# One-core attention with soft experts: row sums folded by a turned VectorE reduce and joined by eight narrow products, with all items placed anew

## The chip, the cores and the metric

One core of one Trainium2 chip runs the whole program. The metric is the device time of one execution in microseconds (us); the median of three runs of the kernel before is 463.78 us (462.85 to 466.7).

## The reference

The inputs are q, k, v of 4 batches x 8 heads x 768 positions x 64, a projection to 6 bits, and the weights of a soft mixture of experts.

```python
q_bits = (einsum('bhsd,dk->bhsk', q, proj) > 0); k_bits = ...      # six bits: a bucket number
mask = q_bucket[:, :, :, None] == k_bucket[:, :, None, :]
scores = where(mask, (q @ k.T) / sqrt(D), -1e9)
attn = exp(scores - max(scores, axis=-1)); attn = attn / (sum(attn, axis=-1) + 1e-9)
x = (attn @ v).transpose(0, 2, 1, 3).reshape(B * S, H * D)          # 3072 x 512
logits = x @ phi                                                    # 32 slots
slot_input = softmax(logits, axis=0).T @ x
slot_out[e] = relu(slot_input[e] @ w1[e]) @ w2[e]                   # 8 experts, 4 slots each
out = softmax(logits, axis=1) @ slot_out
```

The change is about one line of it: `sum(attn, axis=-1) + 1e-9`, the row sums of each head, and the division by them.

## The kernel before, in words

Attention works head by head (32 heads), with keys on the partitions and queries along the free axis, so a row sum is a sum over partitions and over the six key tiles. For head `h` and key tile `i`, in this flow:

- `smax` (TensorE, L692) makes a first product of bits for the mask and the row maximum; `most` (VectorE, L701 and L704) reduces it out of PSUM to maxima `mx`. The PSUM pool `p_sm` of `smax` has two tiles, so `smax` can be two tiles ahead of `most` and no more. A `most` takes one such tile: 512 columns, or two times 256.
- `shift` (VectorE, L730 to L733) turns the maxima of a head into 12 columns of the tile `mz_wide`, and `shift_rows` (TensorE transpose, L740) turns that tile so that ScalarE and a DMA can put it into the operands of the scores.
- `scores` (TensorE, L755) and `exps` (ScalarE, L761) make the exponentials `pt`; three tiles of PSUM hold scores.
- `acc` (GpSimd, L769 and L772) adds up the exponentials of the six key tiles to `acc`, 128 x 768 per head: five additions per head. What is left of the row sum is a sum over the 128 partitions.
- `av` (TensorE, L782) multiplies exponentials and values. Its products are 32 wide in the array, four beside each other; one `av(h, i)` is eight instructions, because an f32 product is two passes.

Two heads form a pair. For pair `p` = (h, h+1) with h even, before:

- `pair_sum` (L794): four products of `ones` (128 x 32) with the two `acc` tiles, 384 columns each, eight instructions side by side as in `av`; then ScalarE adds epsilon into the tile `sm` (L797).
- `pair_turn`: VectorE transposes `sm` in 32 x 32 blocks (L801) and takes the reciprocal of 12 columns (L803).
- `pair_rec`: VectorE transposes the reciprocals back over 384 columns (L807), and four small ScalarE copies (L811) lay them out as `r` for the two heads.
- `pair_log` (TensorE, L819) makes the logits of the pair, `pair_add` (VectorE, L830 and L832) multiplies them with the turned-back reciprocals and adds them up; `pair_x` (VectorE, L841 and L842), twice per pair, turns a head's output and scales it by `r`.

`pair_sum`, `bits`, `pair_log`, `shift` and `pair_x` share two PSUM tiles, `p_mi`. The last pair (heads 30 and 31) takes other functions, `one_sum` (L850) to `one_x`, which sum each head by itself.

The order of the work is written out by hand. Each item (one call such as `av(14, 2)`) has a place, a number: a general place per kind in `WHEN`, counted in key tiles from the start of its head (six per head, so 12 per pair), and places of their own for the first heads in `FIRST` and for the last ones in `LAST`. All items are sorted by place and issued in that order; each engine then runs its instructions strictly in the order of issue. A place is no time: it only decides what stands before what on each engine. After the attention come the experts (L1210 to L1289), which have an order of their own that no place touches.

Of the kernel before, what the change touches and what calls it, by code (L numbers as in the profile page):

```python
# [45 lines left out]
WHEN = {'load': -19.3468,  # L46
 'bits': -14.4383,
 'bits_over': -14.2584,
 'split_hi': -10.9429,
 'split_lo': [-7.9471, -10.3929],  # L50
 'spread': [[-8.8667, -8.6015, -5.9161, -4.1148], [-9.3276, -9.194, -9.0297, -9.106]],
 'load_v': [-2.0731, 0.6585],
 'smax': [[-4.9459, -4.5996, -4.5074, -3.5395, -3.8379, -3.601, -3.1412, -4.194, -2.497, -2.6603, -2.5816, -2.8044], [-7.8073, -7.4789, -7.2707, -6.1194, -5.7614, -1.4853, -1.3463, -5.5604, -1.6131, -0.5258, -0.2808, -0.8326]],
 'scores': [[5.3442, 7.1595, 7.6417, 4.7818, 4.7301, 7.7385, 7.8065, 6.1303, 7.7833, 7.8637, 8.1476, 7.0548], [2.9827, 3.0435, 3.3599, 2.8156, 6.1475, 3.339, 3.3842, 3.4177, 4.8664, 6.3101, 6.3175, 5.5112]],
 'shift': [-2.1809, 1.1337],
 'shift_rows': [-2.0508, 1.4963],
 'acc': [[8.2045, 8.8273, 9.2763, 9.7038, 11.6083], [5.3851, 6.3996, 7.6087, 9.3787, 10.196]],
 'av': [[8.1798, 8.2669, 9.6327, 9.6481, 9.703, 9.8775], [7.1277, 7.2791, 9.6226, 9.7634, 9.8792, 10.1433]],
 'pair_sum': 21.5121,
 'pair_turn': 22.2861,  # L60
 'pair_rec': 22.5427,
 'pair_log': 21.6476,
 'pair_x': [25.4827, 31.869],
 'pair_add': 22.6152,
 'batch_both': 23.9517,
 'batch_max': 28.4907,
 'batch_exp': 29.0783,
 'batch_turn': 33.1628,
 'batch_scale': 38.996,
 'batch_slots': 33.3856,  # L70
 'batch_weigh': 33.2973,
 'batch_share': 33.7326,
 'batch_arrange': 33.8276,
 'load_weights': 32.5147,
 'most': [[-4.2417, -4.1358, -3.3957, -3.7458, -3.1116, -3.8628, -2.4263, -2.4256, -2.7421], [-6.3291, -5.9099, -5.7091, -4.4019, -0.3972, -4.3936, -1.1706, 1.0908, -0.2473]],
 'exps': [[6.8148, 8.101, 6.373, 5.0098, 8.3028, 7.1088, 8.7019, 8.5894, 7.3908], [3.1649, 3.733, 2.9391, 6.3842, 3.7337, 3.5784, 5.6014, 6.3847, 6.3149]]}
# [1278 lines left out]
```

## Time and profile before

| | |
|---|---|
| median of three runs | 463.78 us (462.85 to 466.7) |
| span of the profiled execution | 459.7 us |
| busy: PE / PEld / DVE / ACT / POOL | 444.7 / 277.2 / 336.8 / 275.1 / 350.9 us |
| attention, pair after pair | 54.3 to 388.7 us of the span |
| last pair, and the last logits | 388.7 to 409.5 us |
| experts | 409.5 to 459.7 us |

PE is TensorE's products, PEld its weight loads, DVE is VectorE, ACT ScalarE, POOL GpSimd. A row of the profile gives a line of the kernel, the engine, the operation, the tiles out<-in with their shapes and a count. Busy time of PE is that of pipelined products whose ends are modelled: a PE that is always busy is not yet one at its peak. A time in brackets is the idle time of the engine before the instruction, and behind the arrow stands what ended it.

### The profile page before, as it was taken

Reading aid. Unit: us, or ns where it says so; the run is one execution under the profiler, and the core shown is the slowest. Engines: PE = TensorE matmul, PEld = TensorE weight load, DVE = VectorE, ACT = ScalarE, POOL = GpSimd, SP = SyncE. Lnnn points to the kernel's source line nnn. Section 1 sums busy time; section 2 is a strip of 40 time slices with the busy share of each in tenths; the row PEclk is TensorE's granted clock in tenths of the full one; section 3 lists DMA queues with packets and bytes.
Section 4 is the critical chain, followed back from the end, with each engine's and each line's share of the span. In section 5 each row is a group of like instructions: output and inputs, shape, how many; then the busy total and the mean of one; then the engine's idle time right before and its main releaser. Section 6 shows DMA issues by size and latency. Waiting matters only on the chain. (4 is left out here: it accounts for less than half of the span.)

```text
span 459.7 us, 10940 instructions
## 1 busy us (share of the span) xinstructions
PE 444.7 (97%) x4109; PEld 277.2 (60%) x4109; DVE 336.8 (73%) x670; ACT 275.1 (60%) x572; POOL 350.9 (76%) x220
## 2 busy tenths in 40 slices
PE   8999999999999999999999999999999999879993
PEld 6755656575757575656565656565665754343682
DVE  5967787777798978787889878787988780773142
...
GB/s 207 137 151 148 165 134 153 131 197 164 211 159 190 183 163 209 163 202 171 201 167 187 175 187 190 178 202 169 196 177 112 98 227 404 315 336 355 412 310 274
DMA packets 37704, 93.20 MB, mean 203 GB/s; under 512 B 7106, under 2 KB 13380, under 8 KB 37652
## 3 DMA queue, kind: packets, MB, share of 16 engines
...
q14 instruction: 20, 0.16, 0.1%
q0 software_dynamic: 32, 0.07, 0.0%
HBM read 52.76 MB, written 6.29 MB: 128 GB/s over the span
## 5 line engine op out<-in xcount | busy, mean ns | idle before, releaser
L772 POOL TENSOR_TENSOR acc<-acc,pt 128x768 f32<-128x768 f32 x125 | 229.5, 1838 | 17.4 <-ACT pt L761 11.7
L761 ACT ACTIVATE pt<-st 128x512 f32<-128x512 f32 x288 | 158.2, 598 | 57.2 <-PE st L755 52.8
L755 PE MATMUL st<-XY 128*128 128x512 f32 (+1 forms) x768 | 170.9, 342 | 1.1 <-ACT pt L761 1.1
L704 DVE TENSOR_REDUCE mx<-smx 128x1 f32<-128x512 f32 x192 | 129.3, 687 | 53.0 <-PE smx L692 51.0
L782 PE MATMUL av<-pt,v 128*32 128x384 f32 x1536 | 137.6, 489 | 0.0
L755 PEld LDWEIGHTS st<-XY 128*128 128x128 f32 x768 | 122.2, 190 | 20.0 <-ACT pt L761 3.9
L692 PE MATMUL smx<-XY 96*128 96x256 f32 (+1 forms) x384 | 116.6, 356 | 0.8 <-DVE XY L632 0.3
L692 PEld LDWEIGHTS smx<-XY 96*128 96x128 f32 x384 | 67.7, 190 | 34.8 <-DVE mx L704 12.5
L782 PEld LDWEIGHTS av<-pt,v 128*32 128x32 f32 x1536 | 45.8, 109 | 68.6 <-issue 66.5
L769 POOL TENSOR_TENSOR acc<-pt 128x768 f32<-128x768 f32 x32 | 58.7, 1833 | 12.1 <-ACT pt L761 12.1
L701 DVE TENSOR_REDUCE mx<-smx 128x2 f32<-128x512 f32 x96 | 65.5, 683 | 2.7 <-PE smx L692 2.2
L596 POOL TENSOR_TENSOR w<-raw,w 128x768 fp32r<-128x768 f32 x16 | 35.5, 2222 | 3.8 <-ACT w L592 2.2
L786 ACT COPY avs<-av 128x384 f32<-128x384 f32 x32 | 15.3, 479 | 35.0 <-PE av L782 35.0
L797 ACT ACTIVATE sm<-mi,eps 128x384 f32<-128x384 f32 x15 | 8.7, 582 | 32.0 <-PE mi L794 32.0
L592 ACT CAST w<-raw 128x768 fp32r<-128x768 f32 x30 | 23.6, 834 | 2.4 <-DMA XY<-w 2.1
L609 ACT CAST XY<-w 64x768 fp32r<-64x768 f32 x30 | 23.5, 830 | 0.0
L596 DVE TENSOR_TENSOR w<-raw,w 128x768 fp32r<-128x768 f32 x14 | 16.8, 1203 | 2.7 <-ACT w L592 1.6
L842 DVE TENSOR_TENSOR xq<-mi,r 128x384 f32<-128x384 f32 x30 | 16.7, 558 | 2.1
L841 DVE STREAM_TRANSPOSE mi<-avs 128x384 f32<-128x384 f32 x30 | 17.4, 580 | 0.0
L801 DVE STREAM_TRANSPOSE sm<-sm 128x384 f32<-128x384 f32 x15 | 8.6, 572 | 10.9 <-ACT sm L797 10.9
L1263 PE MATMUL qs<-w 128*32 128x128 f32 x464 | 15.4, 274 | 0.8 <-issue 0.8
L1263 PEld LDWEIGHTS qs<-w 128*32 128x32 f32 x464 | 13.9, 110 | 2.5 <-issue 2.4
...
## 6 DMA issues: line engine op xcount, KB each, us to landing
...
```

Source lines behind the costliest of these rows:

```text
L592: nc.scalar.copy(st[h]["w4"][:, 2 * x], st[h]["raw", x])
L596: (nc.vector if h > 2 and x == 0 else nc.gpsimd).tensor_tensor(out=w[:, 2 * x + 1], in0=st[h]["raw", x], in1=w[:, 2 * x], op=ALU.subtract)
L609: nc.scalar.copy(s["Y"][0:64, x], s["w4"][0:64, 2 * x])
L692: nc.tensor.matmul(pt[:, o:o + b - a], s["Y"][0:96, 0, t * P:(t + 1) * P], s["Y"][0:96, 1, a:b], start=True, stop=True)
L701: nc.vector.tensor_reduce(out=mx[:, n - 1:n + 1], in_=s["sm_ps", n - 1].rearrange("p (a x) -> p a x", a=2), axis=AX.X, op=ALU.max)
L704: nc.vector.reduce_max(out=mx[:, n:n + 1], in_=s["sm_ps", n], axis=AX.X)
L755: nc.tensor.matmul(pt[:, o:o + b - a], x[:, 1, i * P:(i + 1) * P], x[:, 0, a:b], start=first, stop=not first)
L761: nc.scalar.activation(s["P", n // 4][:, 512 * u:512 * u + 512], s["st_ps", n - (n % 4 == 2)], AF.Exp, scale=D ** -0.5)
L769: nc.gpsimd.tensor_tensor(out=s["acc"], in0=pr[:, 0:S], in1=pr[:, S:2 * S], op=ALU.add)
L772: eng.tensor_tensor(out=s["acc"], in0=s["acc"], in1=pr[:, a * S:(a + 1) * S], op=ALU.add)
L782: nc.tensor.matmul(s["av"][2 * e + 32 * c:2 * e + 32 * c + 32, 0:HC], s["v"][:, i, e:e + 32], pr[:, o + c * HC:o + (c + 1) * HC], start=(i ...
L1263: nc.tensor.matmul(pos[i][32 * j:32 * j + 32, 0:w], hTs[g][:, f, 32 * j:32 * j + 32], wt[1, x, 2 * g + f // 4, j][:, (f % 4) * HM + o:(f % ...
```

## The change

The row sums of heads 0 to 29 go another way. A new item `part(h)`, once per head, lets VectorE reduce the 128 x 768 tile `acc` with its 32 x 32 blocks turned: each of the four groups of 32 partitions is summed up, and what comes out is 128 x 24. It is written into columns 12 to 59 of `mz_wide`, 24 for the even and 24 for the odd head; `shift_rows` goes on turning all 72 columns of that tile. `pair_sum` then joins the four groups with a matrix `quarter` (128 x 32, four identities on top of each other): four products of 24 columns and four of 12, which stand in three groups of 12 columns in PSUM and need no ScalarE. `pair_turn` adds epsilon out of PSUM and takes the reciprocals of 36 columns at once; `pair_rec` keeps its transpose back, and its four ScalarE copies and the first transpose go. `add_quarter` makes `quarter` once, in three small GpSimd additions. Some small tiles are put together or share a name.

```diff
+    def add_quarter():
+        nc.gpsimd.tensor_tensor(out=quarter, in0=ident[:, 0:32], in1=ident[:, 32:64], op=ALU.add)
+        for n in (64, 96):
+            nc.gpsimd.tensor_tensor(out=quarter, in0=quarter, in1=ident[:, n:n + 32], op=ALU.add)
...
     def shift(h):
         s = st[h]
-        mz = mz_wide
+        mz = mz_wide[:, 0:2 * NT]
...
-        nc.tensor.transpose(pt[0:72, 0:P], s["mz"], ident)
+        nc.tensor.transpose(pt[0:72, 0:P], mz_wide, ident)
...
+    def part(h):
+        q = st[h - h % 2]
+        q["parts"] = mz_wide[:, 2 * NT:10 * NT].rearrange("p (a j) -> p a j", a=2)
+        nc.vector.tensor_reduce(out=q["parts"][:, h % 2], in_=st[h]["acc"].rearrange("p (j x) -> p j x", x=32),
+                                axis=AX.X, op=ALU.add, apply_transpose=True)
+
     def pair_sum(h):
+        n = NT * 2
         pt = p_mi.tile([P, 512], F32, name="mi")
-        for a in range(2):
-            for c in range(2):
-                r = 64 * a + 32 * c
-                nc.tensor.matmul(pt[r:r + 32, 0:HC], ones, st[h + a]["acc"][:, c * HC:(c + 1) * HC],
-                                 start=True, stop=True)
+        for g in range(4):
+            nc.tensor.matmul(pt[32 * g:32 * g + 32, 0:2 * n].rearrange("p (a j) -> p a j", a=2), quarter,
+                             st[h]["parts"][:, :, g % 2 * n:g % 2 * n + n], start=True, stop=True)
+        for g in range(4):
+            nc.tensor.matmul(pt[32 * g:32 * g + 32, 2 * n:3 * n], quarter,
+                             st[h]["parts"][:, g // 2, g % 2 * n:g % 2 * n + n], start=True, stop=True)
+        st[h]["sum"] = pt[:, 0:3 * n]
+
+    def pair_turn(h):
+        n = NT * 2
+        r = dp.tile([P, 3 * n], F32, name="r", bufs=1)
+        nc.vector.tensor_scalar_add(r, st[h]["sum"], EPS)
+        nc.vector.reciprocal(out=r, in_=r)
+        st[h]["r"] = r[:, 0:2 * n].rearrange("p (a j) -> p a j", a=2)
+        st[h]["rt"] = r[:, 2 * n:3 * n]
+
+    def pair_rec(h):
         st[h]["rs"] = dp.tile([P, HC], F32, name="sm", bufs=1)
-        nc.scalar.activation(st[h]["rs"], pt[:, 0:HC], AF.Identity, bias=eps)
-
-    def pair_turn(h):
-        tt = st[h]["rs"]
-        nc.vector.transpose(tt, tt)
-        r = st[h]["rt"] = dp.tile([P, NT * 2], F32, name="rt", bufs=1)
-        nc.vector.reciprocal(out=r, in_=tt.rearrange("p (j x) -> p j x", x=32)[:, :, 0])
-
-    def pair_rec(h):
-        r = st[h]["rt"]
-        nc.vector.transpose(st[h]["rs"], r[:, :, None].broadcast_to([P, NT * 2, 32]))
-        r2 = st[h]["r"] = dp.tile([P, 2, NT * 2], F32, name="r", bufs=1)
-        for a in range(2):
-            for x in range(2):
-                nc.scalar.copy(r2[64 * x:64 * x + 64, a], r[64 * a:64 * a + 64])
+        nc.vector.transpose(st[h]["rs"], st[h]["rt"][:, :, None].broadcast_to([P, NT * 2, 32]))
...
+        if h < BH - 2:
+            at(s0 + WHEN["part"][x], part, h)
```

All places in `WHEN`, `FIRST` and `LAST` are other numbers. Sorted, they give this order around a pair, with pair (12, 13) as the example:

```
before  TensorE: pair_sum(12) bits(18) av(14,2) pair_log(12) av(14,3) av(14,4) av(14,5) shift_rows(16)
        VectorE: most(16,8) most(16,10) bits_over(18) shift(16) pair_turn(12) pair_rec(12) pair_add(12)
after   TensorE: av(14,2) pair_sum(12) av(14,3) bits(18) av(14,4) pair_log(12) av(14,5) smax(17,0,0) shift_rows(16)
        VectorE: part(13) most(16,10) pair_turn(12) pair_rec(12) bits_over(18) most(16,8) shift(16) pair_add(12)
```

The `part` of an even head stands around the six `av` of an odd head that follow one another, or some items behind them; that of an odd head stands at the end of the next long stretch of `smax` and `scores` (8 of the 14 from head 3 on, just ahead of `av(even, 0)`) or a little later, ahead of its `pair_sum`. Over the whole list TensorE changes between full-width and 32-wide products 119 times before and 116 times after.

## Rows read from the trace of the kernel before

**Rows 1.** The page: the span, then busy us, share and instructions per engine.
```profile
span 459.7 us, 10940 instructions
...
PE 444.7 (97%) x4109; PEld 277.2 (60%) x4109; DVE 336.8 (73%) x670; ACT 275.1 (60%) x572; POOL 350.9 (76%) x220
```

**Rows 2.** Windows from:to, length, busy per engine, clock, DMA: start, pairs, last pair.
```profile
0.00:54.30 54.30, 52.10 (x361) 35.44 (x361) 38.16 (x74) 32.99 (x56) 41.61 (x30) 1.00 0.66 167
54.30:388.66 334.36, 333.44 (x2847) 205.46 (x2850) 266.20 (x521) 219.41 (x458) 301.12 (x183) 1.00 0.69 180
388.66:409.50 20.84, 17.51 (x150) 8.10 (x142) 15.29 (x34) 8.38 (x21) 7.14 (x5) 1.00 0.92 356
```

**Rows 3.** Windows of one pair (same columns): whole period, then its long full-width stretch.
```profile
173.83:197.39 23.56, 23.56 (x195) 14.75 (x194) 18.48 (x35) 15.45 (x31) 20.71 (x12) 1.00 0.74 182
...
185.81:192.24 6.43, 6.43 (x40) 5.45 (x36) 5.60 (x12) 4.78 (x10) 6.27 (x5) 1.00 0.76 184
```

**Rows 4.** Groups by line (busy us, mean ns, idle before): what the change removes.
```profile
L794 PE MATMUL mi<-acc,ones 128*32 128x384 f32 x120 | 12.8, 497 | 0.0
...
L811 ACT COPY r<-rt 64x12 f32<-64x12 f32 x60 | 11.9, 198 | 0.7
...
L797 ACT ACTIVATE sm<-mi,eps 128x384 f32<-128x384 f32 x15 | 8.7, 582 | 32.0 <-PE mi L794 32.0
...
L801 DVE STREAM_TRANSPOSE sm<-sm 128x384 f32<-128x384 f32 x15 | 8.6, 572 | 10.9 <-ACT sm L797 10.9
...
L803 DVE RECIPROCAL rt<-sm 128x12 f32<-128x12 f32 x15 | 3.4, 229 | 0.5
```

**Rows 5.** TensorE's timeline (start, us, count): `av` products of 384 columns.
```profile
176.43 2.12 PE L782 MATMUL av<-pt,v 128*32 128x384 f32 x24
...
181.80 4.08 PE L782 MATMUL av<-pt,v 128*32 128x384 f32 x48
```

**Rows 6.** The chain of waits: 32-wide products of 128 columns in the experts.
```profile
437.58 3.63 PE qs L1263 x128
```

**Rows 7.** Groups by line: prices for the new VectorE instructions, and one that stays.
```profile
L704 DVE TENSOR_REDUCE mx<-smx 128x1 f32<-128x512 f32 x192 | 129.3, 687 | 53.0 <-PE smx L692 51.0
...
L632 DVE TENSOR_SCALAR bt<-mi,con 128x384 fp32r<-128x384 f32 x15 | 10.2, 677 | 2.3 <-PE mi L639 2.2
...
L807 DVE STREAM_TRANSPOSE sm<-rt 128x384 f32<-128x384 f32 x15 | 8.7, 578 | 0.5
...
L730 DVE TENSOR_REDUCE mi<-mx 128x6 f32<-128x12 f32 x31 | 5.4, 174 | 1.3 <-ACT sm L797 0.2
...
L772 DVE TENSOR_TENSOR acc<-acc,pt 128x768 f32<-128x768 f32 x3 | 2.9, 958 | 0.2
...
L1012 DVE RECIPROCAL cs<-cs 128x6 f32<-128x6 f32 x4 | 0.8, 192 | 0.1
...
L859 DVE TENSOR_SCALAR rt<-mi 128x12 f32<-128x12 f32 x1 | 0.2, 170 | 0.1
```

**Rows 8.** VectorE's timeline over that pair: its long waits, and the last step of `shift`.
```profile
186.35 0.69 DVE L704 TENSOR_REDUCE mx<-smx 128x1 f32<-128x512 f32 x1 [1.95 <-PE smx L692]
...
194.32 0.69 DVE L704 TENSOR_REDUCE mx<-smx 128x1 f32<-128x512 f32 x1 [1.06 <-PE smx L692]
...
197.50 0.69 DVE L704 TENSOR_REDUCE mx<-smx 128x1 f32<-128x512 f32 x1 [0.97 <-PE smx L692]
...
200.08 0.16 DVE L733 SCALAR_TENSOR_TENSOR mz<-mi,mz 128x6 f32<-128x6 f32 x1
```

**Rows 9.** TensorE's timeline: `pair_sum`, and the `shift_rows` that follows it.
```profile
197.40 0.85 PE L794 MATMUL mi<-acc,ones 128*32 128x384 f32 x8
...
202.05 0.30 PE L740 MATMUL mi<-ident,mz 128*72 128x128 f32 x1
```

**Rows 10.** GpSimd's timeline: the last additions of the odd head, and the next head's first.
```profile
186.05 5.69 POOL L772 TENSOR_TENSOR acc<-acc,pt 128x768 f32<-128x768 f32 x3
191.70 1.84 POOL L769 TENSOR_TENSOR acc<-pt 128x768 f32<-128x768 f32 x1
```

More of the change, by code (lines that the diff above doesn't have):

```diff
@@ L43 @@
 C_ALL = C_FD + P
[L46 to L73, printed above, removed]
- 'load_weights': 32.5147,
- 'most': [[-4.2417, -4.1358, -3.3957, -3.7458, -3.1116, -3.8628, -2.4263, -2.4256, -2.7421], [-6.3291, -5.9099, -5.7091, -4.4019, -0.3972, -4.3936, -1.1706, 1.0908, -0.2473]],
- 'exps': [[6.8148, 8.101, 6.373, 5.0098, 8.3028, 7.1088, 8.7019, 8.5894, 7.3908], [3.1649, 3.733, 2.9391, 6.3842, 3.7337, 3.5784, 5.6014, 6.3847, 6.3149]]}
@@ new lines @@
+WHEN = {'load': -16.2695,
+ 'bits': -14.2906,
+ 'bits_over': -14.2178,
+ 'split_hi': -9.7035,
+ 'split_lo': [-6.5889, -6.566],
+ 'spread': [[-7.7674, -11.2941, -4.4453, -4.0042], [-8.9583, -8.8975, -8.8868, -8.8244]],
+ 'load_v': [-2.1542, 1.5476],
+ 'smax': [[-4.8292, -3.615, -3.4098, -3.3002, -4.0721, -2.9372, -2.8263, -2.983, -2.4504, -2.6047, -2.3811, -2.7908], [-8.1653, -7.3879, -7.3258, -6.9684, -5.5671, -1.2664, -1.1674, -6.1749, -1.3055, 0.1861, 0.3068, -0.503]],
+ 'scores': [[5.991, 7.6415, 8.0369, 5.111, 4.8744, 8.674, 8.6758, 6.7562, 8.2129, 8.037, 8.3834, 6.6655], [3.338, 3.2724, 3.4096, 3.0392, 5.2003, 3.0568, 3.1604, 3.352, 4.4129, 5.8614, 6.2159, 4.7033]],
+ 'shift': [-2.1709, 1.7327],
+ 'shift_rows': [-2.0724, 1.739],
+ 'acc': [[8.1877, 9.4704, 9.5436, 9.6103, 11.5364], [5.6086, 7.8113, 11.3753, 11.983, 12.0542]],
+ 'av': [[8.7073, 8.7547, 9.6473, 9.6918, 9.7329, 9.812], [7.6017, 7.924, 10.3609, 10.5159, 10.5721, 10.5769]],
+ 'part': [15.0, 14.6],
+ 'pair_sum': 21.6483,
+ 'pair_turn': 21.6658,
+ 'pair_rec': 21.7029,
+ 'pair_log': 21.7636,
+ 'pair_x': [26.6834, 32.1009],
+ 'pair_add': 21.8459,
+ 'batch_both': 25.1587,
+ 'batch_max': 29.2076,
+ 'batch_exp': 33.1012,
+ 'batch_turn': 33.583,
+ 'batch_scale': 46.6232,
+ 'batch_slots': 33.6197,
+ 'batch_weigh': 33.5868,
+ 'batch_share': 33.6423,
+ 'batch_arrange': 33.7695,
+ 'load_weights': 32.5147,
+ 'most': [[-4.2239, -3.1393, -3.0893, -4.003, -2.7662, -2.8724, -2.1952, -2.3528, -2.5772], [-6.8601, -6.2133, -6.1659, -2.4589, 1.3733, -2.3476, 1.3627, 1.6393, 1.6107]],
+ 'exps': [[6.8741, 8.1406, 6.0845, 5.0092, 9.0918, 7.6831, 8.7028, 9.0054, 6.9102], [3.6905, 3.7307, 3.2465, 7.2248, 3.4113, 3.6474, 6.7409, 7.2928, 8.3209]]}
@@ L523, in lsh_attention_soft_moe @@
     nc.scalar.activation(pts[2][:, 512:513], eps, AF.Exp)
+    quarter = cp.tile([P, 32], F32, name="quarter")
     run_n = [cp.tile([P, 1], F32, name=f"run_n{n}") for n in range(2)]
@@ L898, in batch_max @@
         z = bst[b]
-        ml = dp.tile([P, 4], F32, name="ml", bufs=1)
-        mo, sw, mb, z["lb"] = (ml[:, n:n + 1] for n in range(4))
-        z["al"] = dp.tile([P, 1], F32, name="al", bufs=1)
+        ml = dp.tile([P, 8], F32, name="ml", bufs=1)
+        mo, sw, mb, z["lb"], z["al"] = (ml[:, n:n + 1] for n in range(5))
         z["nm"], z["om"] = run_n[b % 2], run_n[1 - b % 2]
@@ L998, in batch_weigh @@
         lg = bst[b]["lt"]
-        m = dp.tile([P, NT], F32, name="cm", bufs=1)
+        m = dp.tile([P, 2 * NT], F32, name="cm", bufs=1)[:, 0:NT]
         cb = call_of(b)
@@ L1079, in lsh_attention_soft_moe @@
     at(last - 12, add_ident)
+    at(4.3, add_quarter)
     for h in range(BH):
```

669 lines of the change are left out of this document (351 added, 318 removed).

## The prediction

> **What bounds the kernel now.** I read the page first: TensorE is busy 97% of the span, VectorE 73%, GpSimd 76%, ScalarE 60% [rows 1]. Such shares mix stages, so the windows come next. Between the first and the last `pair_sum`, 334.36 us, TensorE is busy 333.44 at a clock of 1.00; VectorE has 266.20, GpSimd 301.12, ScalarE 219.41 [rows 2]. The change lies in this stage, for 15 pairs. One pair takes 23.56 us, and TensorE is busy in all of it [rows 3]. So a microsecond of products that goes there is a microsecond off the time, as long as no other engine becomes late; and one that VectorE takes more is free while it fits between its waits. VectorE's waits for products of `smax` are long at three places of a pair: 1.95, 1.06 and 0.97 us [rows 8]. The long full-width stretch has no such place: VectorE is busy 5.60 of 6.43 us, its first 0.54 us passed before the first `smax` was there (185.81 to 186.35), so 0.29 us are free [rows 3, 8].
>
> **TensorE: what `pair_sum` costs.** A wide product costs by its columns: 48 instructions of `av` take 4.08 us and 24 take 2.12, so eight (one `av`, or the old `pair_sum`, of the same shape) take (4.08 - 2.12) / 3 = 0.653 us, and 0.2 us more until the result can be read (0.85 in the row) [rows 5, 9]. The new one is eight products of 24 and 12 columns, two passes each: 16 instructions, each with its own weight load of 32 columns. The trace has no product so narrow. The nearest are the 32-wide ones of 128 columns in the experts, also with a load each: 128 take 3.63 us, 28.4 ns each [rows 6]. Sixteen of them are 0.454 us. That is the upper end, since fewer columns don't cost more. The lower end is columns alone: four side by side pass 128 columns in 4 x 28.4 = 113 ns, 0.89 ns a column, and 2 x (24 + 12) columns then take 0.064 us. I take 0.454: the weight loads stay as many and as wide, and only the columns shrink. TensorE gains 0.653 - 0.454 = 0.20 us per pair, 15 x 0.20 = **3.0 us**; by the lower end 15 x 0.589 = 8.8 us.
>
> The Trainium skill has a rule that speaks against this change's idea ("TensorEngine Tiling (Array Packing)", Instruction Overhead): each matmul has about 60 cycles of overhead, and a free dimension of 1 costs what one of 60 does. By it, as an estimate, 16 instructions at 2.4 GHz would be 0.40 us, and the gain 3.8 us; 28.4 ns per instruction in [rows 6] does not contradict it, and no run here shows a narrower product yet.
>
> **VectorE: what it takes over.** A reduce of 512 columns takes 687 ns and one of 12 columns 174, so 1.03 ns per column, and 768 columns 0.95 us; an addition over 768 columns takes 0.958 [rows 7]. No reduce here is turned. The transposes stay near one column per cycle of that slope (578 ns for 384), so I take 0.96 us for `part`. If turning and reducing were two passes, it would be 0.58 + 384 x 1.03 ns = 0.97, plus 0.95, 1.92 us: the upper end; below 0.95 nothing speaks for. Epsilon is a `TENSOR_SCALAR` of 0.17 us. The reciprocal grows from 192 ns at 6 columns to 229 at 12, 6.2 ns a column, so 36 columns are 229 + 24 x 6.2 = 0.38 us [rows 4, 7]. Away go a transpose (0.57) and a reciprocal of 12 (0.23) [rows 4]. Per pair: 2 x 0.96 + 0.17 + 0.38 - 0.57 - 0.23 = **+1.67 us**. VectorE has 23.56 - 18.48 = 5.08 us free per pair [rows 3]. The even head's `part` stands near the six `av` in a row, where 1.95 us are free [rows 8]. The odd head's stands at the end of the long stretch or behind it: 0.29 us there and the wait of 1.06 us behind it make 1.35, and 0.96 fits. I cost both at nothing; without that cover they cost their lateness.
>
> **ScalarE** loses 0.58 + 4 x 0.198 = 1.37 us per pair [rows 4]. It is busy 15.45 of 23.56 us and bounds nothing [rows 3], so I count nothing.
>
> **Waits that move.** `pair_turn` now reads PSUM itself and, with `pair_rec`, stands ahead of `bits_over`, `most` and `shift`; behind `shift` TensorE waits with `shift_rows` and all products queued after it. Before, `shift` was done at 200.24 and `shift_rows` ran at 202.05, a margin of 1.8 us [rows 8, 9]. After, counted from the first of the 32-wide products: `pair_sum` is readable at 0.65 + 0.45 + 0.20 = 1.31, `pair_turn` ends at 1.86, `pair_rec` (0.58) at 2.44; `bits` is readable at 1.11 + 2 x 0.65 + 0.20 = 2.61; then `bits_over` 0.68, `most` 0.69 and `shift`, three steps of 0.17, end near 4.5. TensorE reaches `shift_rows` after six wide units and the narrow one, 6 x 0.653 + 0.454 = 4.37, and one `smax` more, about 4.6. The margin is 0.1 us: no cost, but nothing left. `pair_sum` waits for the odd `part`; `most` of one tile behind it is the only thing between them on VectorE. The odd `part` waits for GpSimd, whose last addition of that head ended at 191.74 [rows 10], and old `pair_sum` came at 197.40 [rows 9]: 5.7 us, which shrink to almost nothing for the 8 odd heads whose `part` stands at the end of the long stretch (192.24). `part` writes the tile that `shift_rows` reads; both orders keep them apart by several items, so nothing. `add_quarter` falls into the start, where GpSimd is idle 54.30 - 41.61 = 12.7 us [rows 2]: nothing, and at most three times a 768-column addition (1.84, [rows 10]), 5.5 us, if that cover were gone.
>
> **The new order elsewhere.** The changes between full-width and 32-wide products stay as many (119 and 116). In the last pair TensorE is idle 20.84 - 17.51 = 3.3 us [rows 2]: a better order there can gain at most that. I take nothing, and give it 1 us to either side.
>
> **Sum.** The profiled execution is 459.7 us [rows 1]; 459.7 - 3.0 = 456.7. The median of the runs is 4.1 us longer, so 463.8 - 3.0 = **460.8 us**.
>
> **Rivals.**
> (a) *VectorE gets late in the long stretch.* It has 0.29 us free there, so a `part` of 0.96 (or its wait for GpSimd) pushes the `most` behind it by 0.67 us, and TensorE, only two tiles ahead, waits. Eight pairs x 0.67 = 5.4: 463.8 - 3.0 + 5.4 = 466.2; in all 14 pairs 470.2. For it: that stretch, and the margin of 0.1 us above. Against it: two `av` follow at once, during which TensorE needs no `most`.
> (b) *The turned reduce takes two passes, and VectorE becomes the bound: slower.* The place is the odd `part`. It decides from 1.35 us, what is free there. At 1.92 us the excess is 0.57 x 14 = 8.0: 468.8; with the tiles of (a) as well, 1.92 - 0.29 = 1.63 in eight pairs and 0.57 in six, 16.5: 477. I say 473. Against it: transposes and reduces alone both run at one column per 1.03 ns [rows 7].
> (c) *Narrow products cost their columns only.* The gain is 8.8: 455.0. Against it: weight loads of 32 columns stay.
>
> **Chances and range.** The forecast has 0.45 and its own range is 458.5 to 463, from the 1 us of the last pair and some lateness. (a) 0.25, (b) 0.13, (c) 0.10; 0.07 for what a new order does where I read nothing, to both sides. A difference of about 1% (4.6 us) is what a measurement of this kernel can tell from none. Faster by over 1%, below 459.1: (c) 0.10, 0.10 from the forecast's lower part, 0.03 of the rest: 0.23. Slower, above 468.4: (b) 0.13, 0.04 from (a), 0.02: 0.19. Within 1%: 0.58. The range 456 to 469 leaves out most of (b) and (c), about 0.2.
>
> **What would show it.** The products of `pair_sum` spaced by about 28 ns, 16 in 0.45 us; by 4 ns is (c). `part` at 0.96 us; 1.9 is (b). Pairs 23.4 us apart, with TensorE's busy time still the whole window. VectorE near 20.1 us per pair. If (a) holds, weight loads of `smax` wait for `most` or `part` at the end of the long stretch, and `part` waits for GpSimd's `acc`. A `shift_rows` that waits for `shift` shows the lost margin. The forecast falls if pairs come no closer, or if the last pair or the start moves by over 2 us.

## The result and the profile after

The changed kernel takes 467.40 us (median of 20 runs, 465.45 to 470.98); the kernel before took 464.12 on the same chip (20 runs). The ratio is 1.0078, interval 1.0056 to 1.0099: slower by 0.8%, 3.3 us. The forecast was 460.8, faster by 3.0, in its own range 458.5 to 463.

The two traces lie further apart than the medians: 468.4 against 459.7 us of span [rows 1], as the profiled execution of after was one of its long ones (470.51) and that of before, by its span, a short one. What follows compares traces stage by stage and takes the medians for the verdicts.

The page of after, as [rows 1]:

```profile
span 468.4 us, 11186 instructions
...
PE 443.7 (95%) x4229; PEld 276.4 (59%) x4229; DVE 365.2 (78%) x700; ACT 259.9 (55%) x497; POOL 353.6 (75%) x223
```

VectorE does 28.4 us more and ScalarE 15.2 less; forecast were 15 x 1.67 = 25 and 15 x 1.37 = 20.6. TensorE does a little less work, but in a span 8.7 us longer: it now waits (PE's busy time also counts stretches at a lower clock as busy). The groups by line of the new instructions, as [rows 4, 7] (busy us, mean ns, idle before):

```profile
L832 DVE TRANSPOSE_TENSOR_REDUCE mz<-acc 128x24 f32<-128x768 f32 x30 | 29.0, 968 | 4.9 <-PE st L795 4.9
...
L850 DVE RECIPROCAL r<-r 128x36 f32<-128x36 f32 x15 | 5.7, 378 | 0.5
...
L849 DVE TENSOR_SCALAR r<-mi 128x36 f32<-128x36 f32 x15 | 2.9, 193 | 9.4 <-PE mi L842 9.4
```

`part` costs 0.968 us (forecast 0.96), the reciprocal of 36 columns 0.378 (0.38), epsilon 0.193 (0.17). TensorE's timeline at a `pair_sum`, against [rows 9]:

```profile
104.02 0.24 PE L839 MATMUL mi<-mz,quarter 128*32 128x24 f32 x8
104.08 0.23 PE L842 MATMUL mi<-mz,quarter 128*32 128x12 f32 x8
104.15 0.83 PE L822 MATMUL av<-pt,v 128*32 128x384 f32 x8
```

The next product starts 0.13 us behind the first narrow one, where 0.454 was forecast. So the narrow products are far cheaper than forecast, TensorE should gain 0.653 - 0.13 = 0.52 us a pair, 7.8 us in all, and the kernel is slower all the same. Windows of three pairs, from one `pair_sum` to the next (columns as in [rows 2]): a plain pair; one in which a batch of logits ends; the pair behind such a one.

```profile
80.43:104.02 23.59, 23.55 (x206) 14.64 (x202) 20.13 (x38) 14.36 (x27) 20.66 (x12) 1.00 0.60 156
127.58:153.94 26.36, 25.01 (x255) 15.33 (x250) 23.14 (x49) 15.19 (x30) 21.97 (x14) 1.00 0.68 175
153.94:178.52 24.58, 23.55 (x206) 14.51 (x206) 22.29 (x41) 16.04 (x33) 22.85 (x17) 1.00 0.65 170
```

The plain pair is as long as before (23.56 [rows 3]) though its work is shorter; in the two others TensorE is idle by 1.35 and 1.03 us, at a full clock of 1.00. The table cuts the span of each trace into the time to the first `pair_sum`, the mean length of 7 plain pairs, of the 3 batch pairs, of the 3 pairs behind them, and the rest (the 14th pair to the end). The runs e1 to e15 are told below. All are starts of the first `pair_sum` product, read from the timelines; in the kernels with the new places it stands one `av` (0.65 us) later in its pair, which moves that much from the rest to the start.

| kernel | start | plain | batch | behind | rest | span | median of runs |
|---|---|---|---|---|---|---|---|
| before | 54.32 | 23.55 | 25.44 | 23.53 | 93.65 | 459.7 | 464.1 |
| after | 57.19 | 23.70 | 26.46 | 24.59 | 92.17 | 468.4 | 467.4 |
| e1 new code, old places | 59.94 | 23.58 | 26.30 | 23.71 | 91.38 | 466.4 | 467.9 |
| e2 old code, new places | 53.99 | 24.73 | 26.31 | 25.55 | 99.84 | 482.5 | 485.3 |
| e3 after, weights later | 54.23 | 23.58 | 26.55 | 24.61 | 93.63 | 466.4 | 467.8 |
| e4 after without `part` | 53.93 | 23.71 | 25.48 | 24.57 | 93.26 | 463.3 | 465.9 |
| e5 e1, mended | 56.53 | 23.35 | 26.61 | 24.30 | 90.99 | 463.7 | 466.2 |
| e6 after, mended | 54.53 | 24.22 | 29.45 | 23.90 | 93.26 | 477.4 | 479.4 |
| e8 e1, other mends | 54.36 | 23.05 | 25.93 | 26.78 | 92.67 | 466.5 | 467.3 |
| e10 before, mends of e8 | 54.33 | 24.32 | 25.44 | 26.84 | 93.66 | 475.1 | 474.1 |
| **e11 e1, two mends** | 54.66 | 23.05 | 25.75 | 23.68 | 91.60 | 455.9 | **459.8** |
| e12 before, mends of e11 | 54.57 | 23.79 | 25.44 | 23.73 | 93.50 | 462.1 | 466.0 |
| e15 after, `smax` later | 54.29 | 23.67 | 25.74 | 25.07 | 92.07 | 464.5 | 466.3 |

Between the traces of before and after, the start gives +2.9, the plain pairs 7 x 0.15 = +1.1, the batch pairs 3 x 1.02 = +3.1, those behind 3 x 1.06 = +3.2, the rest -1.5: 8.8 of 8.7. The start belongs to that execution: e3 and e4, with the same TensorE items up to there, have 54.23 and 53.93. In after's trace TensorE stood 1.68 us for a DMA (`XY<-mr`) until 51.53, and then its granted clock was at 0.50, the lower of its two levels (1.2 GHz), for 3.42 us in which it was busy throughout; at the full clock that work would have taken half as long, so this clock is 1.7 us of the 2.9 (an estimate from the row):

```profile
51.53 0.98 PE L795 MATMUL st<-XY 128*128 128x512 f32 x4 [1.68 <-DMA XY<-mr]
...
52.27:55.69 3.42, 3.42 (x13) 2.97 (x12) 2.17 (x3) 1.20 (x2) 3.34 (x2) 0.50 0.44 113
```

Three losses are left: plain pairs that don't get shorter, batch pairs, pairs behind.

**What the two longer kinds wait for.** In the pair behind a batch, VectorE's timeline and TensorE's loads:

```profile
153.72 0.41 DVE L1018 COPY run_x<-mi 128x256 f32<-128x256 f32 x1
154.05 0.34 DVE L1054 TENSOR_REDUCE cs<-lacc 128x6 f32<-128x192 f32 x1
154.43 0.73 DVE L1055 TENSOR_SCALAR cs<-cs 128x6 f32<-128x6 f32 x1
...
155.87 0.18 DVE L849 TENSOR_SCALAR r<-mi 128x36 f32<-128x36 f32 x1
156.09 0.38 DVE L850 RECIPROCAL r<-r 128x36 f32<-128x36 f32 x1
156.57 0.58 DVE L856 STREAM_TRANSPOSE sm<-r 128x384 f32<-128x384 f32 x1
157.07 0.64 DVE L672 TENSOR_SCALAR bt<-mi,con 128x384 fp32r<-128x384 f32 x1
157.63 0.68 DVE L744 TENSOR_REDUCE mx<-smx 128x1 f32<-128x512 f32 x1
...
158.75 0.17 DVE L773 SCALAR_TENSOR_TENSOR mz<-mi,mz 128x6 f32<-128x6 f32 x1
...
159.06 0.27 PE L780 MATMUL mi<-ident,mz 128*72 128x128 f32 x1 [1.03 <-DVE mz L773]
```

VectorE works without a pause from 153.72 to 158.92: the end of the old batch (L1018, `batch_slots`, and L1054 to L1056, `batch_share`) comes first, then `pair_turn`, `pair_rec`, `bits_over`, a maximum and `shift`. TensorE stands 1.03 us at `shift_rows`. This is the margin of 0.1 us of the prediction, gone. A batch pair has two places. The first, in the first of the three, is a DMA:

```profile
122.10 1.40 SPq L508 DMA_DIRECT2D w<-w  x1
123.60 0.98 SPq L640 DMA_DIRECT2D XY<-w  x1
124.62 3.87 SPq L640 DMA_DIRECT2D XY<-bt  x4
...
132.40 0.47 PE L732 MATMUL smx<-XY 96*128 96x512 f32 x1 [1.28 <-DMA XY<-bt]
```

The odd head's bits (`XY<-bt`) are issued behind a 512 KB load of expert weights on SP's queue, and its first `smax`, which the new order puts ahead of `shift_rows`, waits 1.28 us for them. The second is VectorE behind the six `av`: `part` (L832), the steps of `batch_max` (L947 to L953) and `split_lo` (L636, half of an addition whose other half GpSimd does) meet. In the first batch pair only a weight load waits there, 0.50 us; in the other two TensorE itself waits for a maximum, 1.58 and 0.79 us.

```profile
137.31 0.97 DVE L832 TRANSPOSE_TENSOR_REDUCE mz<-acc 128x24 f32<-128x768 f32 x1
...
138.21 0.50 DVE L947 TENSOR_REDUCE ml<-dl 64x1 f32<-64x384 f32 x1
...
139.74 1.07 DVE L636 TENSOR_TENSOR w<-raw,w 128x768 fp32r<-128x768 f32 x1 [0.15 <-DMA XY<-bt]
...
141.47 0.19 PEld L732 LDWEIGHTS smx<-XY 96*128 96x128 f32 x1 [0.50 <-DVE mx L744]
...
237.04 2.56 DVE L636 TENSOR_TENSOR w<-raw,w 128x768 fp32r<-128x768 f32 x1
...
240.25 0.50 PE L732 MATMUL smx<-XY 96*128 96x512 f32 x1 [1.58 <-DVE mx L744]
```

### The profile page after: what moved, and what is told of

It is laid out like the page before. It is cut to its first block, busy times and chain, and to the rows that moved or that the text cites. A ratio compares the mean times of both kernels' runs of the same rounds, so it can differ in the third digit from the quotient of the medians.

```text
span 468.4 us, 11186 instructions
## 1 busy us (share of the span) xinstructions
PE 443.7 (95%) x4229; PEld 276.4 (59%) x4229; DVE 365.2 (78%) x700; ACT 259.9 (55%) x497; POOL 353.6 (75%) x223
## 4 chain that ended last, share of the span: by engine, by line
PE 74%; DVE 9%; DMA 8%; SPq 5%; issue 2%; ACT 1%; DVEq 0%
PE st L795 25%; PE av L822 19%; PE smx L732 15%; SPq L640 4%; DMA XY<-bt 4%; PE qs L1310 3%; PE qh L1257 3%; DVE mx L744 2%; PE mi L780 1%; DMA w<-w 1%; PE mi L679 1%; DVE w L636 1%; DMA XY<-mr 1%; PE av L583 1%; PE mi L1012 1%
## 5 line engine op out<-in xcount | busy, mean ns | idle before, releaser
L812 POOL TENSOR_TENSOR acc<-acc,pt 128x768 f32<-128x768 f32 x125 | 233.3, 1868 | 30.4 <-ACT pt L801 24.0
L801 ACT ACTIVATE pt<-st 128x512 f32<-128x512 f32 x288 | 160.6, 597 | 86.3 <-PE st L795 83.3
L795 PE MATMUL st<-XY 128*128 128x512 f32 (+1 forms) x768 | 172.9, 343 | 1.9 <-DMA XY<-mr 1.7
L822 PE MATMUL av<-pt,v 128*32 128x384 f32 x1536 | 142.1, 489 | 0.0
L795 PEld LDWEIGHTS st<-XY 128*128 128x128 f32 x768 | 126.4, 191 | 22.5 <-issue 4.5
L732 PE MATMUL smx<-XY 96*128 96x512 f32 (+1 forms) x384 | 120.2, 361 | 6.2 <-DMA XY<-bt 2.8
L822 PEld LDWEIGHTS av<-pt,v 128*32 128x32 f32 x1536 | 43.2, 110 | 62.4 <-issue 60.0
L636 POOL TENSOR_TENSOR w<-raw,w 128x768 fp32r<-128x768 f32 x16 | 34.4, 2149 | 0.0
L832 DVE TRANSPOSE_TENSOR_REDUCE mz<-acc 128x24 f32<-128x768 f32 x30 | 29.0, 968 | 4.9 <-PE st L795 4.9
L636 DVE TENSOR_TENSOR w<-raw,w 128x768 fp32r<-128x768 f32 x14 | 21.3, 1523 | 1.1 <-DMA XY<-bt 0.9
L783 ACT CAST mr<-mi 12x128 fp32r<-12x128 f32 x31 | 7.9, 255 | 11.6 <-PE mi L780 8.7
```

What stands on the lines that cost most here:

```text
L636: (nc.vector if h > 2 and x == 0 else nc.gpsimd).tensor_tensor(out=w[:, 2 * x + 1], in0=st[h]["raw", x], in1=w[:, 2 * x], op=ALU.subtract)
L732: nc.tensor.matmul(pt[:, o:o + b - a], s["Y"][0:96, 0, t * P:(t + 1) * P], s["Y"][0:96, 1, a:b], start=True, stop=True)
L795: nc.tensor.matmul(pt[:, o:o + b - a], x[:, 1, i * P:(i + 1) * P], x[:, 0, a:b], start=first, stop=not first)
L801: nc.scalar.activation(s["P", n // 4][:, 512 * u:512 * u + 512], s["st_ps", n - (n % 4 == 2)], AF.Exp, scale=D ** -0.5)
L812: eng.tensor_tensor(out=s["acc"], in0=s["acc"], in1=pr[:, a * S:(a + 1) * S], op=ALU.add)
L822: nc.tensor.matmul(s["av"][2 * e + 32 * c:2 * e + 32 * c + 32, 0:HC], s["v"][:, i, e:e + 32], pr[:, o + c * HC:o + (c + 1) * HC], start=(i ...
```

## The experiments

Four theories. *Code*: the new instructions themselves cost the time. *Places*: the new order does, and the new code in another order gains. Within the second, *bits land late* (the DMA above) and *VectorE is late* (what it does ahead of a maximum or a shift).

**e1 and e2: one half of the change each.** e1 is the new code in the places of the kernel before; e2 the old code in the new places.

```diff
 # e1: WHEN, FIRST, LAST of before, and
+ 'part': [16.1, 14.5],
- 'pair_turn': 22.2861,  'pair_log': 21.6476
+ 'pair_turn': 21.64,    'pair_log': 21.71
+ ('part', -3): -5.1,  ('pair_x', -6, 1): -4.97
 # e2: functions of before; WHEN, FIRST, LAST of after without part and add_quarter
- ('pair_rec', -4): -2.2968
+ ('pair_rec', -4): -3.535
```

> The new code of the row sums in the old places: every item stands where it stood before, the parts are put into VectorE's waits (even heads behind the six av in a row, odd heads into the 1.06 us wait behind av(even, 0) and av(even, 1)), pair_turn stands just ahead of bits_over and pair_log one av later. Theory 'places' (the narrow products take 0.13 us instead of 0.65, and the loss comes from the new places: bits that land late, and a VectorE order without margin): pairs 23.56 - 0.52 = 23.04 us apart, 15 x 0.52 = 7.8 us off the kernel before, about 456.3. Rival 'code' (VectorE's 1.67 us more per pair take the gain back wherever the items stand): pairs 23.5 us or more apart, 463 to 466.

> The old code of the row sums in the new places (no part, wide pair_sum, ScalarE's copies; pair_rec of the last such pair stands ahead of pair_x). Theory 'places': the places alone cost, and nothing of the narrow products comes back: 467.4 + 7.8 = 475, at least above 470. Rival 'code': without the 1.67 us on VectorE the new places are as good as the old, 463 to 466.

e1: 467.89 us, ratio 1.0068 (1.0041 to 1.0094); e2: 485.28, 1.0442 (1.0413 to 1.047). Both lie above what either theory expected. Neither half is good alone, so the medians settle nothing: the new places serve only the new code, and in e2 VectorE waits 33.3 us for ScalarE's `sm` (17.85 of it at once, at 415 us), which the new code doesn't have. But e1's first pairs take 23.00, 23.15 and 23.16 us, 0.4 to 0.5 less than before: where nothing is late, the gain of the narrow products arrives. What e1 loses lies elsewhere, first of all in a start that is 5.6 us longer. VectorE's `part` of head 0, then TensorE's loads, then a window of TensorE's busy time and clock:

```profile
46.34 0.98 DVE L827 TRANSPOSE_TENSOR_REDUCE mz<-acc 128x24 f32<-128x768 f32 x1 [3.49 <-POOL acc L807]
...
47.95 0.19 PEld L727 LDWEIGHTS smx<-XY 96*128 96x128 f32 x1 [3.80 <-DVE mx L739]
...
48.77:52.19 3.42, 3.42 (x11) 2.75 (x10) 1.60 (x5) 1.57 (x3) 1.20 (x1) 0.50 0.09 23
```

I had put it ahead of GpSimd's last addition of that head; VectorE stood for 3.49 us, with all maxima queued behind it, TensorE's loads for 3.80 and its products for 3.37. Then the granted clock stood at 0.50 for 3.42 us, as in the start of after: about 1.7 of the 5.6 us.

**e3: are the bits late because of the weights?** In after, the weight loads go behind the bits on SP.

```diff
- 'load_weights': 32.5147,
+ 'load_weights': 33.25,
```

> The changed kernel with one number changed: the loads of weights (512 KB each) are issued behind the moves of the odd heads' bits instead of just ahead of them. Theory 'bits land late': smax of odd heads no longer waits for the DMA of the bits, pairs during the loads fall from 24.0 to 24.6 us to 23.6, about 4 us off the changed kernel's 467.4: 463. Rival 'VectorE is late': nothing changes, 466.5 to 468.

467.82 us, ratio 1.0068 (1.004 to 1.0096): no gain. Late plain pairs fall from 24.00 and 24.12 to 23.61, so the bits did cost there, but batch pairs stay at 26.55. In the first of them the wait has only changed its cause:

```profile
135.88 2.56 DVE L662 TENSOR_TENSOR w<-raw,w 128x768 fp32r<-128x768 f32 x1 [0.15 <-DMA XY<-bt]
...
139.09 0.50 PE L758 MATMUL smx<-XY 96*128 96x512 f32 x1 [1.56 <-DVE mx L770]
...
135.78 1.84 POOL L662 TENSOR_TENSOR w<-raw,w 128x768 fp32r<-128x768 f32 x1
```

`split_lo` on VectorE takes 2.56 us here: it begins 0.10 us behind GpSimd's half of it and ends 0.82 us behind that half's end (137.62).

**e4: after without `part`** for heads 2 to 29, whose pairs then use the sums of the first pair.

```diff
-            at(s0 + WHEN["part"][x], part, h)
+            at(s0 + WHEN["part"][x], part if h < 2 else no_part, h)
```

> The changed kernel without the turned reduces of heads 2 to 29 (part of the computation is left out: the row sums of those heads are those of the first pair). It takes 28 x 0.97 = 27 us off VectorE. Rival 'VectorE is late': pairs that are not held by a DMA fall from 23.57 to about 23.1 us, and the kernel to about 460. Theory 'bits land late': those pairs may shorten, but the ones with loads of weights stay at 24 to 24.6, and the time stays above 464.

465.92 us, ratio 1.0034 (1.0014 to 1.0055). Batch pairs fall from 26.46 to 25.48: without `part` no maximum is late there, but in the first of them the wait that shrinks is the one for the bits (1.28 to 0.28 us). Plain pairs (23.71) and pairs behind (24.57) don't move. So 27 us less work on VectorE (28 x 0.968) give back 1.5 us of the median, and two of the three losses are not `part`'s. Nor is the third its alone: in e15 below, with `part`, the first two batch pairs take 25.38 and 25.49 us, and `split_lo` 1.06 and 1.04; where `split_lo` takes 2.55 or 2.56 behind `part` (after, e3), such a pair takes 26.8 to 26.9. So what comes late in the runs shown is `part` and `split_lo` together.

**e5 and e6: moving VectorE's items away.** e5 mends e1, e6 mends after.

```diff
 # e5 against e1
+ ('part', 0): 19.3,  ('part', 1): 21.0
+ 'batch_max': 31.3,  'batch_exp': 31.55,  'bits_over': -14.372
 # e6 against after
+ 'pair_rec': 21.93,  'pair_add': 22.65,  'batch_max': 31.2,  'batch_exp': 31.4,  'batch_turn': 32.75,
+ 'batch_weigh': 32.95,  'batch_share': 33.56,  'load_weights': 33.25
```

> The change's code in the places of the kernel before, as in e1_code_old_places, with three groups of items moved: the first two heads' part (0 from 16.1 to 19.3, 1 from 20.5 to 21.0), batch_max and batch_exp from 28.49 and 29.08 to 31.3 and 31.55 (behind the shift of the odd head instead of inside the long stretch, next to part and split_lo), and bits_over from 21.74 to 21.63, ahead of pair_turn. 'VectorE is late' (each loss of e1 is a VectorE instruction ahead of a max or a shift that TensorE waits for): e1's first row sums come back from 59.94 to about 54.5-55.5, its three batch pairs fall from 26.2-26.5 to 25.0-25.4, the plain pairs stay at 23.0-23.2; with e1's median 467.9 that is -5 -3 -1 = 458 to 460 us, faster than both. 'Code' (the new code itself costs what the places do not explain): the lost time stays in the pairs and the median stays above 464. 'Bits land late': pairs late in the run that stood at 23.9-24.4 in e1 fall to about 23.2 because the bits go 0.57 us sooner; if the bits are late for another reason they stay.

> The changed kernel with its VectorE items beside the row sums and the batches moved: pair_rec from 21.70 to 21.93 and pair_add from 21.85 to 22.65 (behind the shift), batch_max and batch_exp from 29.21 and 33.10 to 31.2 and 31.4, batch_turn, batch_weigh and batch_share from 33.58, 33.59 and 33.64 to 32.75, 32.95 and 33.56, load_weights at 33.25. 'VectorE is late': the pair after a batch falls from 24.6 to about 23.6 or less (batch_share no longer stands ahead of the shift), a batch pair from 26.4-26.9 to about 25.4, a plain pair from 23.6 to 23.1-23.4; sum -3 -3 -3 = 457 to 461 us. 'Places elsewhere' (the new places of smax, most, scores and exps themselves hold the pairs at 23.6): plain pairs stay at 23.6 and only the six batch pairs gain, 461 to 463 us. 'Bits land late': nothing here but load_weights touches the bits, so the gain is that of e3, and the median stays at 466-468 us.

e5: 466.17, ratio 1.004 (1.0012 to 1.0068); e6: 479.44, 1.032 (1.029 to 1.0351). Both expectations failed. In e5 the first three plain pairs stand at 22.97 to 22.99, but batch pairs stay at 26.6: moving `batch_max` behind the shift moves the wait with it, as VectorE is busy 24.16 of 26.31 us in such a pair, and pairs behind a batch grow to 24.30. In e6 pairs behind a batch do fall (24.59 to 23.90), while all others grow: `pair_add` behind a `smax` stands ahead of a maximum, and TensorE waits for that (0.73 us at 132.75, in the first batch pair). The other long waits of that pair are for maxima again (0.76 us at 141.04, 1.00 at 148.90) and of `scores` for `exps` (1.48 at 151.35): 4.0 us with the first, where after has 1.35.

**e7: the price of the narrow products.** e1 with the 16 instructions issued four times over.

```diff
+        for _ in range(4):
             for g in range(4):
                 nc.tensor.matmul(pt[...], quarter, st[h]["parts"][...], start=True, stop=True)
             ...   # and the four of 12 columns, in the same loop
```

> As e1_code_old_places, with the sixteen narrow products of each pair issued four times over into the same place (each starts its sums anew, so the last counts): 48 instructions more per pair, 15 times. By the forecast's price of 28.4 ns an instruction a pair grows by 1.36 us (23.1 to 24.4) and the median by 20 us over e1 (to about 488 us). If four column groups run side by side and the instructions cost their columns alone (0.13 us for sixteen, about 8 ns each), a pair grows by 0.39 us (to about 23.5) and the median by about 6 us (to about 474 us).

473.44 us, 5.6 above e1's 467.9. The first two pairs grow from 23.00 and 23.15 to 23.44 and 23.61: 0.45 us for 48 instructions, 9.4 ns each. TensorE's timeline, the first sixteen and what follows all four:

```profile
83.78 0.26 PE L835 MATMUL mi<-mz,quarter 128*32 128x24 f32 x8
83.86 0.23 PE L838 MATMUL mi<-mz,quarter 128*32 128x12 f32 x8
83.93 0.24 PE L835 MATMUL mi<-mz,quarter 128*32 128x24 f32 x8
...
84.50 0.88 PE L674 MATMUL mi<-raw,pb 128*32 128x384 f32 x8
```

Sixteen take 0.15 us. By the price of the forecast the pair would have grown by 1.36. This settles the price: 0.15, not 0.454.

The Trainium skill ("TensorEngine Tiling (Array Packing)", Instruction Overhead) gives each matmul about 60 cycles; by it sixteen would be 0.40 us, an estimate. The runs disagree: 0.13 to 0.15 us, 9.4 ns each, with four products beside each other in the array, and the measurement decides.

**e8, e9 and e10: the waits of e1 and e5, one by one.** `part` of heads 0 and 1 in gaps of VectorE, the weights behind the bits, `batch_share` behind the shift, `pair_add` later. e9 adds e5's `batch_max` and `batch_exp`; e10 puts those mends that it can take into the kernel before.

```diff
 # e8 against e1 (e10: the last five lines, in the kernel before)
+ ('part', 0): 20.3,  ('part', 1): 21.3
+ ('acc', 1, 5): 20.15
+ 'load_weights': 33.45
+ 'batch_share': 33.955
+ 'batch_arrange': 33.96
+ 'pair_add': 22.9
```

> The change's code in the places of the kernel before, as e1_code_old_places, with four mends, each for a wait that the traces of e1 and e5 show: the first two parts in gaps of VectorE (head 0 at 20.3, head 1 at 21.3, with acc of head 1's last key tile at 20.15); load_weights at 33.45, behind the odd head's bits on SP; batch_share and batch_arrange at 33.955 and 33.96, behind the shift; pair_add at 22.9 for 22.62. 'Places' (the code is worth about 0.5 us a pair, and each loss of e1 and e5 is a place): first row sums at 54.3 to 55, plain pairs 23.0 to 23.1 to the end (none at 23.8 to 24.4), pairs after a batch 23.1 to 23.6, batch pairs still 26.2, as VectorE has no idle time left there; sum 457 to 460 us, faster than both kernels. 'Code': it stays above 463.

> As e8_third_places, with batch_max and batch_exp at 31.3 and 31.55 (behind the odd head's shift) instead of 28.49 and 29.08. If a batch pair is long because three VectorE items meet in the long stretch (split_lo, part, batch_max), it falls from 26.2 to about 25.4 and the whole by 2 us. If VectorE is simply full over the whole batch pair (24 us of work in 26), the wait moves behind the shift and the pair stays at 26.2 to 26.4.

> The kernel before, code and places, with those mends of e8 that it can take (acc of head 1's last key tile, load_weights, batch_share, batch_arrange, pair_add): what e8 would owe to the mends alone. In the trace of before neither the bits nor the batch's shares are waited for, so 'places' expects no change: 463.5 to 465 us, pairs at 23.5 and 25.4. If it falls to 461 or less, the gain of e8 is the mends' and not the code's.

e8: 467.32, ratio 1.0071 (1.004 to 1.0101); e9: 468.34, 1.008 (1.0052 to 1.0108); e10: 474.07, 1.0216 (1.0176 to 1.0256). In e8 the start is back at 54.36 and all seven plain pairs at 22.97 to 23.25: both causes were right. But the pairs behind a batch go to 26.78, in e10 too. VectorE, then TensorE's loads, then a window, in e8:

```profile
155.97 0.56 DVE L872 TENSOR_TENSOR lacc<-mi,sm 128x384 f32<-128x384 f32 x1 [2.43 <-POOL ct L1064]
...
157.19 0.19 PEld L729 LDWEIGHTS smx<-XY 96*128 96x128 f32 x1 [2.41 <-DVE mx L741]
...
157.82:161.23 3.41, 3.41 (x16) 1.95 (x18) 3.15 (x7) 2.12 (x4) 3.41 (x2) 0.50 0.02 6
```

`pair_add` (L872) writes the buffer `lacc` in which GpSimd still works on the shares of the old batch; later shares made VectorE stand for 2.43 us, and the maxima behind it. TensorE's products stood for 1.97 us, and after that its granted clock was 0.50 for 3.41 us (the window above), about 1.7 us more. My mend made that loss. In e9 the later `batch_max` brings nothing once more (batch pairs 26.17 against 25.93).

**e11 and e12: without that mend.** e11 is e8 with `batch_share`, `batch_arrange` and `pair_add` back in the places of before; e12 is the kernel before with the two mends it can take.

```diff
 # e11 against e1
+ ('part', 0): 20.3,  ('part', 1): 21.3,  ('acc', 1, 5): 20.15,  'load_weights': 33.45
 # e12 against before
+ ('acc', 1, 5): 20.15,  'load_weights': 33.45
```

> As e8_third_places with batch_share, batch_arrange and pair_add back at 33.73, 33.83 and 22.62, so that only the start (parts of the first two heads, acc of head 1's last key tile) and load_weights differ from e1_code_old_places. In e8 VectorE waited 7.3 us in three turns for GpSimd's ct before pair_add's first sum, and the pair behind each batch took 26.8 us against 23.7 in e1. 'Places': the start stays at 54.4, plain pairs at 23.0, batch pairs at 25.7 to 26.3, pairs behind a batch fall back to 23.7; e8's 467.3 less 3 times 3.1 = 458 us, faster than both kernels. 'Code': it stays above 463.

> The kernel before, code and places, with the two mends of e11 that it can take (load_weights at 33.45, acc of head 1's last key tile at 20.15): the control for e11. 'Places' and the reading that the gain is the code's: within 1 us of before, 463.5 to 465.5, its pairs at 23.5, 25.4 and 23.5. If it falls to 461 or less, e11's gain is the mends'.

e11: **459.77 us, ratio 0.9915 (0.9885 to 0.9944): faster than both kernels.** e12: 466.03, 1.0062 (1.0033 to 1.0092): the mends alone bring no gain, so e11's is that of the new code (with `pair_turn` and `pair_log` moved for it, which e12 has not; e12 came out 0.5 us above its expectation, and two of its plain pairs hold stops of 0.3 and 0.6 us in `scores`). What it is made of shows in plain pairs when TensorE's products are measured from the start of one to the start of the next, so that they add up to the pair (mean of three pairs without a wait for a DMA, us):

| | `pair_sum` | `smax` | `scores` | `av` | all others | pair |
|---|---|---|---|---|---|---|
| before | 0.67 | 4.83 | 8.53 | 8.13 | 1.4 | 23.54 |
| after | 0.12 | 5.00 | 8.86 | 8.21 | 1.4 | 23.57 |
| e11 | 0.15 | 4.80 | 8.53 | 8.13 | 1.4 | 22.98 |

In e11 everything but `pair_sum` takes what it took before, and the pair gains about what `pair_sum` gains. In after `scores`, `smax` and `av` together take 0.6 us more, and the gain is gone. Two windows of e11, a plain pair and a batch pair:

```profile
77.73:100.70 22.97, 22.97 (x203) 14.67 (x202) 19.80 (x37) 14.28 (x27) 21.71 (x12) 1.00 0.60 146
123.94:149.62 25.68, 24.86 (x252) 15.46 (x251) 23.88 (x49) 16.03 (x32) 22.41 (x14) 1.00 0.67 173
```

And the two `part` of the start, with no wait of their own, in gaps of VectorE:

```profile
50.14 0.97 DVE L829 TRANSPOSE_TENSOR_REDUCE mz<-acc 128x24 f32<-128x768 f32 x1
51.51 0.69 DVE L741 TENSOR_REDUCE mx<-smx 128x1 f32<-128x512 f32 x1 [0.40 <-PE smx L729]
...
53.63 0.97 DVE L829 TRANSPOSE_TENSOR_REDUCE mz<-acc 128x24 f32<-128x768 f32 x1
```

**e13 to e17: which of the new places holds a plain pair at 23.6?** e13 puts after's early `pair_rec` and `pair_add` into e11, e14 its early first `smax` of the odd head; e15 takes that `smax` out of after. e16 and e17 put whole groups of after's places into e11.

```diff
 # e13                                      # e14: first entry of 'smax', odd heads
+ 'pair_rec': 21.735,  'pair_add': 21.83    - -7.8073   + -8.06
 # e15, against after: the same entry, and the weights
- -8.1653   + -8.05
+ 'load_weights': 33.25
 # e16: smax, most, shift, shift_rows of after   # e17: scores, exps, acc, av of after
```

> As e11_fourth_places, with VectorE's items of the row sums put at the pair's start as the changed kernel has them: pair_rec from 22.54 to 21.735, ahead of the bits and the shift, pair_add from 22.62 to 21.83, right behind the shift. 'VectorE's order at the start of a pair': plain pairs grow from 23.0 to 23.4-23.6, as the shift, then the first maxima come 0.6 to 1.1 us later, and the median goes from 459.8 to 464-467. 'TensorE's order' (smax ahead of shift_rows, the av products split) or places elsewhere: plain pairs stay at 23.0 to 23.1 and the median within 1 us of e11, the pairs behind a batch aside.

> As e11_fourth_places, with the odd head's first smax at -8.06 for -7.81, ahead of shift_rows on TensorE as the changed kernel has it. 'TensorE's order': plain pairs grow from 23.0 to 23.4-23.6, as it then waits for the odd head's bits ahead of shift_rows. 'VectorE's order': they stay at 23.0 to 23.1, median 459 to 461.

> The changed kernel with the odd head's first smax at -8.05 for -8.17, behind shift_rows, and load_weights at 33.25 as in e3_weights_behind_bits. 'TensorE's order': plain pairs fall from 23.6 to about 23.1 and the median by about 4 us below e3, to 463-464. 'VectorE's order' or places elsewhere: plain pairs stay at 23.6, median 467 to 468 as e3.

> As e11_fourth_places, with the places of smax, most, shift and shift_rows from the changed kernel. 'Places of the maxima': in the changed kernel a 512 wide smax takes 439 ns in the mean against 410 in e11 and waits for a maximum four times a pair against three; plain pairs grow from 23.0 to 23.4-23.6 and the median from 460 to 466. 'Places of the scores and av products': plain pairs stay at 23.0 to 23.1.

> As e11_fourth_places, with the places of scores, exps, acc and av from the changed kernel (its av products split about the row sums). 'Places of the scores and av products': plain pairs grow from 23.0 to 23.4-23.6. 'Places of the maxima': they stay at 23.0 to 23.1, median 459 to 461. If both runs grow, the two groups only fit together with each other, and no single item is to blame.

e13: 460.77 us (0.9942, interval 0.9917 to 0.9966), plain pairs 23.11; e14: 460.40 (0.9928, 0.9898 to 0.9959), 23.08 to 23.32 and one of 24.16; e15: 466.27 (1.0061, 1.0027 to 1.0094), plain 23.67. So neither of the two single moves is the cause; e15 only puts a wait of 0.16 us at `shift_rows` in place of the earlier `smax`. e16 (488.44) and e17 (604.19) break the order so far that they tell nothing of a plain pair but that the groups only fit together. What the traces show is the kind of loss. TensorE's full-width `smax` products in a plain pair, by shape, after and then e11:

```profile
L732 PE MATMUL smx<-XY 96*128 96x512 f32 x12 | 5.3, 439 | 0.0
```

```profile
L729 PE MATMUL smx<-XY 96*128 96x512 f32 x13 | 5.3, 410 | 0.0
```

Each takes 439 ns in the mean against 410: more of them begin behind a short stop for a maximum (`PEld smx` waits for `mx` or `mz` three times in the plain pair of after, 0.5 to 0.6 each, and twice in e11's). By the table under e11 `smax` is only 0.2 of the 0.6 us; `scores`, which wait in the same queue behind such stops, are 0.3, `av` 0.1. Which item is to blame stays open.

## Why the prediction was wrong

- **TensorE's term was mis-sized.** It took 28.4 ns an instruction [rows 6], as weight loads stay as wide; sixteen measured 0.13 to 0.15 us, not 0.454 (rows at 104.02 of after; e7). The row was read rightly but is no price for an instruction: its 0.89 ns a column, four products beside each other, is nearly that of `av` (0.653 us for 2 x 384 columns, 0.85), so that it is bound by its 128 columns. The lower end (columns alone, 0.064) was the nearer one, though 0.13 to 0.15 is twice that. The gain on TensorE was 0.5 us a pair, not 0.2: rival (c), with 0.589, was close.
- **"The new order elsewhere: nothing" failed,** and this is the step that turned the sign. With the same code, plain pairs take 23.70 in the new places and 23.05 in e11; pairs behind a batch 24.59 and 23.68; batch pairs 26.46 and 25.75. Against the kernel before, e11 gains and after loses; e11's batch pairs (25.75 against 25.44) and pairs behind (23.68 against 23.53) are still longer than before, and its gain is in the plain pairs and the end. I had counted the switches between product widths, and read nothing about what an order does to VectorE.
- **"VectorE fits, so it costs nothing" held for plain pairs and failed for batch pairs.** The 5.08 us free came from one plain pair [rows 3]. The trace of before has a batch pair with half as much: 25.41 - 22.58 = 2.83 us.

```profile
124.90:150.31 25.41, 25.41 (x244) 15.68 (x243) 22.58 (x47) 16.90 (x36) 22.61 (x15) 1.00 0.73 184
```

  Three pairs of this kind were in the trace, and I read none. In e4, without `part`, they are 1.0 us shorter, though part of that is the bits and part `split_lo`, which GpSimd holds up by up to 1.6 us. This is the mechanism of rival (a), VectorE late behind `part`, but at another place: not the odd head's `part` in plain pairs, but the even head's in batch pairs.
- **The margin of `shift_rows`.** Worked out as 0.1 us for a plain pair and costed at nothing; true there (in the plain pair shown `shift` ends 3.55 us behind the first narrow product and `shift_rows` starts at 3.80, without a wait), but in a pair behind a batch VectorE starts late and TensorE waits 1.03 us. e13 shows that an early `pair_rec` alone doesn't do it: in e11's places the pair has room for it.
- **VectorE's prices were right** (0.968, 0.378, 0.193), and the turned reduce costs one pass: rival (b) falls. Whether ScalarE's loss of work brought anything, no run tests by itself. `add_quarter` shows no cost in the start (54.23 in e3, 54.32 before).
- **The end.** From the 14th pair on, after gains 1.5 us, a little over the 1 us that was given to the last pair; 0.65 of it is only the later place of `pair_sum`. e11, in the old places, gains 2.05 there.

The time of 467.4 lay inside the stated range of 456 to 469, and close to rival (a)'s 466.2, but by luck, as a sum of two errors: a gain on TensorE of about 7.5 us (15 x 0.5) where 3.0 was forecast, and losses of 10.8 (467.4 - 464.1 + 7.5) which the forecast held at nothing. The forecast was a gain; the kernel got slower, because of the second.
